# Two PSUM tiles for a pair's block products, a new list of steps, and the low parts of x2's sums on GpSimd

## The chip, the core and the metric

The kernel runs on one core of a Trainium2 chip. The metric is the device time in microseconds (us) from the first to the last instruction of the core and what lies around it; smaller is better. In the text PE is TensorE, DVE is VectorE, ACT is ScalarE, POOL is GpSimd, and SP is the engine whose queue issues every DMA of this kernel.

## What is computed

```python
def _moe_ref(x, w_in, w_out):            # 4608 x 512, 512 x 2048, 2048 x 512
    h = x @ w_in
    g = h - np.tanh(h)
    return g @ w_out

def _moe2_ref(x, w_in, w_out, a, b):     # same shapes
    h = x @ w_in
    h2 = h * h
    P = a[0] + a[1] * h + a[2] * h2 + a[3] * h2 * h
    Q = 1.0 + np.abs(b[0]) * np.abs(h) + np.abs(b[1]) * h2
    return (P / (Q + 1e-06)) @ w_out

x = attention(q, k, v)                   # linear attention, 8 x 8 heads, 576 x 64
return _moe2_ref(x=_moe_ref(x=x, ...), ...)
```

## The kernel before

Every large product is done in three matmuls of fp32r operands: each operand is split into a high part (a copy rounded to fp32r) and a low part (what is left), and high by high, high by low and low by high are added up in PSUM.

**The first phase** (the loop over `STEPS` = 144 steps, 9 blocks of 512 tokens with 16 slices of d_ff each) computes attention and the first feed-forward layer. A step does 12 matmuls for `hps`, then tanh on ACT, the subtraction on DVE, the high part on ACT (line 327), the low part on POOL (line 331), and two steps later 12 matmuls into four banks `acc`. The attention of the next block runs beside it in small pieces, among them a chain of K's column maxima (DVE, a DMA to HBM and back, DVE, ACT's exp, PE's `kvps`, line 490). At the end of a block its result x2 is cut into quadrants, and `x2_units` (lines 346 to 378) forms the seven sums that a 2 x 2 block product by Strassen-Winograd needs. Each of the seven is split: ACT copies the high part (line 356), an engine subtracts it from the sum in place to get the low part (line 357), and SP stores both to `x2d` in HBM (line 359). One piece of that generator runs per step. Line 357 is on DVE for units 1, 5, 7, 6 and 4, and on POOL for 3 and 2.

**The second phase** (the loop over `PAIRS` = 72 pairs of slices, 8 pairs to a block of tokens) computes the second layer. A pair `i` needs seven block products `P1` to `P7` (`product`, lines 814 to 833), each of 6 matmuls of 256 columns. They share one PSUM tile `zy` of two banks with four halves: product 4 in half 0, products 1, 6, 7 on top of each other in half 1 (one running sum), product 2 in half 2, products 5 and 3 on top of each other in half 3. ACT takes a copy of half 1 after product 1 (`s1`), after 6 (`s2`) and after 7 (`s3`, into `top`). DVE then forms the two slices of h: `add2` reads halves 0 and 3 plus `top` (side B of the pair), and `add1`, after product 3, reads halves 2 and 3 plus the two copies in `sums` (side A). The rational function of h follows for each side: `ab`, `sq`, `n1`, `rs`, `r2` on ACT, `q`, `st`, `en`, `gh`, `gl` on DVE, `m1`, `m2`, `m3` on POOL, `n0` on POOL (A) or ACT (B). `gh` and `gl` are the high and low parts of the result, and four groups `G` (`GA0` to `GA3`, `GB0` to `GB3`, 3 matmuls of 512 columns each) multiply them into the banks `acc0` to `acc3`. After 8 pairs `lv0` to `lv3` copy the banks out (DVE) and store them.

What sets the order in the second phase is the table `ORDER` (lines 28 to 39), written out by hand: each entry is a step and its lag. In round `i` the loop at line 992 emits the steps in that order, each for pair `i - lag`; every engine executes its own instructions in the order in which they are emitted. Waits between engines are set by the framework: a write to a PSUM tile waits for the reads of that tile that were emitted before it. `zy` has one buffer, so product 1 of a pair waits for all reads of the pair before.

The operands of the products stand in a ring: the weights of a pair are loaded after product 3 of the pair four before it (`ring`), and the units of x2 are loaded by `load_unit` at the last pair of a block, each into the place of the unit that the product just done has freed:

```python
if q == KF // 2 - 1:
    load_unit(*((j + 1, u + 3) if u < 4 else (j + 2, u - 4)))
```

`u` is the product's place in `UNITS = (1, 5, 2, 6, 7, 4, 3)`. So product 2 (`u` = 2) loads the unit that product 4 of the next block reads. The sums of the last block of x2 are formed in the second phase, one piece per round (`prep`, line 998).

Of the kernel before, what the change touches and what calls it, by code (L numbers as in the profile page):

```python
# [8 lines left out]
F32 = mybir.dt.float32  # L9
F32R = mybir.dt.float32r  # L10
# [5 lines left out]
ALU = mybir.AluOpType  # L16
AX = mybir.AxisListType

P = 128
# [10 lines left out]
    for name, lag in (  # L30
        x.split(".")
        for x in """
    P1.0 n0B.1 glB.2 m3A.2 P5.0 s1.0 lv2.3 stA.2 P2.0 abB.1 m1B.1 lv3.3 P6.0 enA.2 sqA.1 GB0.2 qB.1 s2.0
    n0A.1 GB2.2 ghA.2 rsB.1 P4.0 m2B.1 glA.2 r2B.1 P7.0 abA.1 GB1.2 stB.1 m3B.1 GB3.2 s3.0 qA.1 n1A.1
    GA1.2 add2.0 rsA.1 GA2.2 m1A.1 enB.1 GA0.2 sqB.0 ghB.1 P3.0 n1B.0 m2A.1 lv0.2 GA3.2 lv1.2 r2A.1
    add1.0
    """.split()
    )
]
LAGS = max(lag for _, lag in ORDER)  # L40
# [3 lines left out]
def attention_moe_moe2_kernel(ctx, tc, q, k, v, w1, w2, w3, w4, ca, cb, out):  # L44
# [145 lines left out]
    HALF = NB // 2  # L190
# [94 lines left out]
    def ring(i):  # L285

        h, l = wsl["a", i % (WS)]
        f = 2 * (i % (KF // 2))
        d = parked["a", f]
        SP.dma_start(out=f32(h), in_=d[:, 0:4])  # L290
        SP.dma_start(out=f32(l)[:, 0:3], in_=d[:, 4:7])

    def combo(i, m, c):

        u = UNITS.index(m)
        t = wsl["a", i % WS][u // 4][:, u % 4, :]
        return t[:, c * P:(c + 1) * P], t[:, HALF + c * P:HALF + (c + 1) * P]
# [45 lines left out]
    def two(t):  # L343
        return t.rearrange("p (c x) -> p c x", c=2)

    def x2_units(j, k0, k1, ta, tb, new_hi):

        x11, x12, x21, x22 = k0[:, :, LO], k0[:, :, HI], k1[:, :, LO], k1[:, :, HI]
        ta, tb = two(ta), two(tb)

        def minus(o, a, b):
            POOL.tensor_tensor(out=o, in0=a, in1=b, op=ALU.subtract)

        def split(m, x, eng):
            hi = two(new_hi())
            ACT.copy(out=hi.bitcast(F32R), in_=x)
            eng.tensor_tensor(out=x.bitcast(F32R), in0=x, in1=f32(hi), op=ALU.subtract)
            for i, t in enumerate((hi, x)):
                SP.dma_start(out=two(x2d[j][:, 2 * UNITS.index(m) + i]), in_=f32(t))

        minus(ta, x12, x11)
        yield
        split(1, x11, DVE)
        minus(tb, x22, ta)
        yield
        split(5, ta, DVE)
        minus(x12, x22, x12)
        yield
        split(3, x22, POOL)
        yield  # L370
        split(7, x12, DVE)
        minus(ta, x21, tb)
        yield
        split(2, x21, POOL)
        yield
        split(6, tb, DVE)
        yield
        split(4, ta, DVE)
# [319 lines left out]
    with tc.manual_schedule():  # L698
# [104 lines left out]
        def unit(j, m):  # L803
            k = 2 * (len(UNITS) * j + UNITS.index(m))
            return [units[(k + i) % len(units)] for i in range(2)]

        def load_unit(j, u):
            if j < NBLK:
                for i, t in enumerate(unit(j, UNITS[u])):
                    SP.dma_start(out=f32(t), in_=x2d[j][:, 2 * u + i])  # L810

        pair, tile = {}, {}

        def product(i, m):

            if m == 1:
                pair[i] = ps_p.tile([P, 4, HALF], F32, tag="zy", name="zy")
            o = pair[i][:, {1: 1, 6: 1, 7: 1, 4: 0, 2: 2, 5: 3, 3: 3}[m], :]
            j, q = i // (KF // 2), i % (KF // 2)
            hi, lo = unit(j, m)  # L820
            for c in range(2):
                wh, wl = combo(i, m, c)
                xc = slice(c * HALF, (c + 1) * HALF)
                for k, (w, x) in enumerate(((wh, hi), (wh, lo), (wl, hi))):
                    PE.matmul(  # L825
                        o, w, x[:, xc], start=m in (1, 5) and c == k == 0, stop=c == 1 and k == 2,
                        skip_group_check=True,
                    )
            u = UNITS.index(m)
            if q == KF // 2 - 1:  # L830
                load_unit(*((j + 1, u + 3) if u < 4 else (j + 2, u - 4)))
            if u == len(UNITS) - 1 and i + WS < PAIRS:
                ring(i + WS)

        def snap(i, k):
            ACT.copy(out=top if k == 2 else sums[:, k * HALF:(k + 1) * HALF], in_=pair[i][:, 1, :])  # L836

        def add1(i):
            zy = pair.pop(i)
            t = tile[2 * i] = {}  # L840
            new(t, "h")
            DVE.tensor_tensor(out=t["h"], in0=zy[:, 2:4, :].rearrange("p r x -> p (r x)"), in1=sums, op=ALU.add)  # L842

        def add2(i):
            zy = pair[i]
            t = tile[2 * i + 1] = {}
            new(t, "h")
            DVE.tensor_tensor(
                out=two(t["h"]), in0=zy[:, 0:4:3, :], in1=top.unsqueeze(1).to_broadcast([P, 2, HALF]), op=ALU.add
            )  # L850
# [51 lines left out]
        for n in range(STEPS):  # L902
# [9 lines left out]
            if n == last + 10:  # L912
# [10 lines left out]
                sums = xup.tile([P, NB], F32, tag="sums", name="sums")  # L923
                top = xup.tile([P, HALF], F32, tag="top", name="top")
# [10 lines left out]
            t = gp.tile([P, NB], F32, tag="t", name="t", bufs=1)  # L935
# [42 lines left out]
        steps = {f"P{m}": lambda i, m=m: product(i, m) for m in UNITS}  # L978
        steps |= {"s1": lambda i: snap(i, 0), "s2": lambda i: snap(i, 1), "s3": lambda i: snap(i, 2), "add1": add1, "add2": add2}
# [49 lines left out]
```

## Time and profile before

| what | value |
|---|---|
| median of 3 runs | 1789.42 us (1786.61 to 1790.46) |
| profiled execution | 1785.54 us, span 1783.8 us |
| PE busy | 1676.2 us, 94% of the span |
| DVE, ACT, POOL busy | 1177.7, 1010.1, 983.2 us |
| PE's clock over the span | 0.990 of full speed |
| first phase | from 0 to about 921 us |
| second phase | from about 921 us to the end |

A busy PE in this profile is not a PE at its peak, because matmuls are pipelined and their ends are modelled. The rate is read from the distance between starts; a gap stands in brackets behind a row with the engine and line that ended it.

### The profile page before, as it was taken

The page shows a single profiled execution, that of the slowest core. Times are in us where ns is not written, and L with a number is a line of the kernel's source. Part 1 is how long each engine was busy: PE and PEld are TensorE (multiplying, and loading weights), DVE is VectorE, ACT ScalarE, POOL GpSimd, SP SyncE. Part 2 cuts the span into 40 slices and gives each one's busy share as a digit, 9 for nine tenths or more (in the row PEclk, how much of TensorE's full clock was granted, in tenths as well). Part 3 has the DMA queues.
Part 4 walks back from the last instruction along what each step waited for, and adds up shares of the span by engine and source line. Part 5 has one row for each costly group of instructions (what it writes and reads, how often), then busy time and mean ns, then how long its engine had stood idle before and what let it go on. Part 6 is the DMA issues. An engine that isn't in the chain of part 4 may idle for free.

```text
span 1783.8 us, 25853 instructions
## 1 busy us (share of the span) xinstructions
PE 1676.2 (94%) x8776; PEld 1410.2 (79%) x8776; DVE 1177.7 (66%) x1921; ACT 1010.1 (57%) x1825; POOL 983.2 (55%) x830
## 2 busy tenths in 40 slices
PE   5899999999999999999998999999999999999998
PEld 4677787888878787888877878888888788888886
DVE  8987657666657666552216786767776767676776
ACT  5675444445444444443327766666666666666664
POOL 3223434443434444352427877777777777777775
PEclk8999999999999999999999999999999999999999
DMA  8553637565563737350786876666575748575630
GB/s 222 177 170 101 192 108 206 143 185 167 166 192 116 212 111 217 96 172 17 233 309 205 288 227 215 199 203 217 187 236 167 254 154 269 161 249 171 198 121 24
DMA packets 246115, 323.67 MB, mean 181 GB/s; under 512 B 119008, under 2 KB 176352, under 8 KB 236768
## 3 DMA queue, kind: packets, MB, share of 16 engines
q1 hardware_dynamic: 245984, 322.03, 57.7%
q8 instruction: 69, 1.13, 0.3%
q14 instruction: 62, 0.51, 0.1%
HBM read 249.04 MB, written 72.93 MB: 180 GB/s over the span
## 4 chain that ended last, share of the span: by engine, by line
PE 74%; DVE 12%; ACT 6%; DMA 3%; issue 3%; SPq 1%; POOL 1%; DVEq 0%; POOLq 0%; ACTq 0%
PE zy L825 21%; PE acc L80 11%; PE acc L81 11%; PE acc L82 11%; PE hps L80 5%; PE hps L82 5%; PE hps L81 5%; DVE h L842 3%; DMA ke<-kd 2%; ACT sums L836 2%; PE kvps L490 1%; DVE m L147 1%; DVE ke L473 1%; ACT m L133 1%; DVE m L134 1%
## 5 line engine op out<-in xcount | busy, mean ns | idle before, releaser
L331 POOL TENSOR_TENSOR gl<-t,gh 128x512 fp32r<-128x512 f32 x128 | 171.8, 1342 | 352.4 <-ACT gh L327 323.4
L327 ACT CAST gh<-t 128x512 fp32r<-128x512 f32 x128 | 79.6, 622 | 309.3 <-PE acc L82 129.2
L883 POOL TENSOR_TENSOR n<-n,r 128x512 f32<-128x512 f32 x144 | 186.8, 1297 | 101.6 <-ACT r L880 96.1
L883 POOL TENSOR_TENSOR n<-n,h 128x512 f32<-128x512 f32 x144 | 186.9, 1298 | 74.2 <-ACT n L863 62.6
L883 POOL TENSOR_TENSOR n<-n,n 128x512 f32<-128x512 f32 x144 | 186.4, 1294 | 5.7
L836 ACT COPY sums<-zy 128x256 f32<-128x256 f32 x144 | 53.6, 372 | 224.3 <-PE zy L825 222.2
L939 DVE TENSOR_TENSOR t<-hps,t 128x512 f32<-128x512 f32 x128 | 87.4, 683 | 119.9 <-ACT t L936 119.1
L936 ACT ACTIVATE t<-hps 128x512 f32<-128x512 f32 x144 | 85.8, 596 | 98.6 <-PE hps L82 80.6
L872 DVE SCALAR_TENSOR_TENSOR a<-h,absb,a 128x512 f32<-128x512 f32 x144 | 108.1, 751 | 46.0 <-ACT a L857 45.8
L886 DVE SCALAR_TENSOR_TENSOR a<-a,r 128x512 f32<-128x512 f32 x144 | 100.0, 694 | 47.6 <-ACT r L880 47.4
L842 DVE TENSOR_TENSOR h<-zy,sums 128x512 f32<-128x512 f32 x72 | 49.7, 690 | 104.8 <-ACT n L867 94.1
L863 ACT ACTIVATE n<-h,coef 128x512 f32<-128x512 f32 x144 | 117.1, 813 | 0.0
L889 DVE SCALAR_TENSOR_TENSOR a<-a,n 128x512 f32<-128x512 f32 x144 | 100.0, 694 | 9.5 <-POOL n L883 3.5
L893 DVE CAST gh<-a 128x512 fp32r<-128x512 f32 x144 | 99.1, 688 | 7.4
L896 DVE TENSOR_TENSOR gl<-a,gh 128x512 fp32r<-128x512 f32 x144 | 98.8, 686 | 7.0
L875 ACT ACTIVATE r<-a,bias_q 128x512 f32<-128x512 f32 x144 | 98.7, 686 | 4.0 <-DVE a L872 3.9
L857 ACT ACTIVATE a<-h,coef 128x512 f32<-128x512 f32 x144 | 98.8, 686 | 2.4 <-DVE gl L896 2.3
L598 POOL TENSOR_TENSOR qe<-qe,qs 128x512 f32<-128x512 f32 x36 | 38.0, 1056 | 99.4 <-DVE qs L597 99.4
L880 ACT ACTIVATE r<-r 128x512 f32<-128x512 f32 x144 | 90.3, 627 | 2.3
L860 ACT ACTIVATE h<-h 128x512 f32<-128x512 f32 x144 | 89.8, 624 | 0.8 <-DMA xl<-x2d 0.8
L869 POOL TENSOR_SCALAR n<-h,coef 128x512 f32<-128x512 f32 x72 | 55.5, 770 | 50.7 <-DVE a L889 50.7
L490 PE MATMUL kvps<-vt,ke 128*128 128x130 f32 x320 | 47.7, 300 | 27.1 <-ACT ke L483 25.8
(313 smaller groups left out, 5188.9 us busy)
## 6 DMA issues: line engine op xcount, KB each, us to landing
u<-x2d SPq DMA_DIRECT2D x78, 256.0 KB, 5.3
raw<-in_moe_w_in_dram SPq DMA_DIRECT2D x32, 512.0 KB, 4.5
raw<-in_moe_w_out_dram SPq DMA_DIRECT2D x32, 512.0 KB, 4.4
x2d<-e SPq DMA_DIRECT2D x56, 256.0 KB, 3.0
wa0h<-wa0d SPq DMA_DIRECT2D x9, 1024.0 KB, 5.1
wa1h<-wa2d SPq DMA_DIRECT2D x9, 1024.0 KB, 5.1
wa2h<-wa4d SPq DMA_DIRECT2D x9, 1024.0 KB, 5.1
wa3h<-wa6d SPq DMA_DIRECT2D x9, 1024.0 KB, 7.9
```

What stands on the lines that cost most here:

```text
L80: PE.matmul(o, lhi, rhi, start=start, stop=False)
L81: PE.matmul(o, lhi, rlo, start=False, stop=False)
L82: PE.matmul(o, llo, rhi, start=False, stop=stop)
L331: eng.tensor_tensor(out=gl, in0=g, in1=f32(gh), op=ALU.subtract)
L825: PE.matmul(o, w, x[:, xc], start=m in (1, 5) and c == k == 0, stop=c == 1 and k == 2, skip_group_check=True,)
L842: DVE.tensor_tensor(out=t["h"], in0=zy[:, 2:4, :].rearrange("p r x -> p (r x)"), in1=sums, op=ALU.add)
L863: ACT.activation(out=new(t, "n1"), in_=t["h"], func=AF.Identity, scale=a3, bias=a2)
L872: DVE.scalar_tensor_tensor(out=t["a"], in0=t["h2"], scalar=b1, in1=t["a"], op0=ALU.mult, op1=ALU.add)
L883: return lambda t: POOL.tensor_tensor(out=t[a], in0=t[a], in1=t[b], op=op)
L886: DVE.scalar_tensor_tensor(out=t["a"], in0=t["a"], scalar=ONE_EPS, in1=t["r"], op0=ALU.add, op1=ALU.mult)
L889: DVE.scalar_tensor_tensor(out=t["a"], in0=t["a"], scalar=2.0, in1=t["n0"], op0=ALU.subtract, op1=ALU.mult)
L893: DVE.tensor_copy(out=t["g"][0], in_=t["a"])
```

## The change

- The tile `zy` becomes two tiles of one bank each: `y` with product 4 in half 0 and products 5 and 3 in half 1, and `z` with product 2 in half 0 and products 1, 6, 7 in half 1. Products 2 and 4 change banks by this. `add2` reads `y` alone.
- `add1` becomes two instructions of 256 columns: `a11` (z plus the first copy) and `a12` (y plus the second).
- `ORDER` is laid out anew. The products now run 1, 6, 5, 4, 7, 2, 3 instead of 1, 5, 2, 6, 4, 7, 3. The eight groups stand in four twos, behind products 1, 7, 2 and 3. `GA3` and `GA0` have lag 3.
- Line 357 is on POOL for all seven units, in both phases.
- `prep` runs in every fourth round from round 3 on, instead of in each round from round 2 on. The load of the first block's last unit stands ahead of a weight load between the phases.

```diff
-    P1.0 n0B.1 glB.2 m3A.2 P5.0 s1.0 lv2.3 stA.2 P2.0 abB.1 m1B.1 lv3.3 P6.0 enA.2 sqA.1 GB0.2 qB.1 s2.0
...
+    P1.0 ghB.2 m3A.2 GA3.3 s1.0 glB.2 GA0.3 n1A.1 stA.2 P6.0 m1B.1 sqA.1 lv1.3 enA.2 P5.0 s2.0 ghA.2
...
-        def split(m, x, eng):
+        def split(m, x):
             hi = two(new_hi())
             ACT.copy(out=hi.bitcast(F32R), in_=x)
-            eng.tensor_tensor(out=x.bitcast(F32R), in0=x, in1=f32(hi), op=ALU.subtract)
+            POOL.tensor_tensor(out=x.bitcast(F32R), in0=x, in1=f32(hi), op=ALU.subtract)
...
             if m == 1:
-                pair[i] = ps_p.tile([P, 4, HALF], F32, tag="zy", name="zy")
-            o = pair[i][:, {1: 1, 6: 1, 7: 1, 4: 0, 2: 2, 5: 3, 3: 3}[m], :]
+                pair[i] = tuple(ps_p.tile([P, 2, HALF], F32, tag=tag, name=tag) for tag in "yz")
+            y, z = pair[i]
+            o = {1: z[:, 1], 6: z[:, 1], 7: z[:, 1], 2: z[:, 0], 4: y[:, 0], 5: y[:, 1], 3: y[:, 1]}[m]
...
-        def add1(i):
-            zy = pair.pop(i)
-            t = tile[2 * i] = {}
-            new(t, "h")
-            DVE.tensor_tensor(out=t["h"], in0=zy[:, 2:4, :].rearrange("p r x -> p (r x)"), in1=sums, op=ALU.add)
+        def add1(i, k):
+            t = tile.setdefault(2 * i, {})
+            h = t["h"] if t else new(t, "h")
+            c = slice(k * HALF, (k + 1) * HALF)
+            y, z = pair[i]
+            DVE.tensor_tensor(out=h[:, c], in0=y[:, 1] if k else z[:, 0], in1=sums[:, c], op=ALU.add)
...
-        ring(WS - 1)
         load_unit(0, 6)
+        ring(WS - 1)
...
-            if i >= LAGS:
+            if i % 4 == 3:
                 next(prep, None)
```

PE, second phase, a pair of the last block, before: the last group of the pair ahead (bank `acc_16533`), then the products 1 and 5 (one row, from `xh`), the products 2 and 6 (one row, from `xl`), and the first group behind them.

```order
L80 MATMUL acc_16533<-wb2h,gh 128x512
L81 MATMUL acc_16533<-wb2l,gh 128x512
L82 MATMUL acc_16533<-wb2h,gl 128x512
L825 MATMUL zy<-xh,wa3h 128x256 x12
L825 MATMUL zy<-xl,wa3h 128x256 x12
L80 MATMUL acc_16493<-wb2h,gh 128x512
```

The same place after: the group `GB0`, product 1, the groups `GA3` and `GA0`, product 6, product 5.

```order
L80 MATMUL acc_16697<-wb2h,gh 128x512
L81 MATMUL acc_16697<-wb2l,gh 128x512
L82 MATMUL acc_16697<-wb2h,gl 128x512
L826 MATMUL z<-xh,wa3h 128x256 x6
L80 MATMUL acc_16689<-wb2h,gh 128x512
L81 MATMUL acc_16689<-wb2l,gh 128x512
L82 MATMUL acc_16689<-wb2h,gl 128x512
L80 MATMUL acc_16697<-wb2h,gh 128x512
L81 MATMUL acc_16697<-wb2l,gh 128x512
L82 MATMUL acc_16697<-wb2h,gl 128x512
L826 MATMUL z<-xl,wa3h 128x256 x6
L826 MATMUL y<-xh,wa3h 128x256 x6
```

Two groups now stand between product 1 and the next product that writes the same tile, where another product of the same tile stood; between product 3 and the next product 1 there are two groups (of which the last is shown) instead of one.

DVE, one pair of the second phase, before (line 848 is `add2`, 842 `add1`, 872 `q`, 886 `st`, 889 `en`, 893 `gh`, 896 `gl`):

```order
L848 TENSOR_TENSOR h<-zy,top 128x512
L889 SCALAR_TENSOR_TENSOR a<-a,n_16585 128x512
L893 CAST gh<-a 128x512
L842 TENSOR_TENSOR h<-zy,sums 128x512
L896 TENSOR_TENSOR gl<-a,gh 128x512
L886 SCALAR_TENSOR_TENSOR a<-a,r 128x512
L889 SCALAR_TENSOR_TENSOR a<-a,n_16620 128x512
L872 SCALAR_TENSOR_TENSOR a<-h_16674,absb,a 128x512
L893 CAST gh<-a 128x512
L896 TENSOR_TENSOR gl<-a,gh 128x512
L886 SCALAR_TENSOR_TENSOR a<-a,r 128x512
L872 SCALAR_TENSOR_TENSOR a<-h_16731,absb,a 128x512
```

One pair on DVE after (line 844 is `a11` and `a12`):

```order
L848 TENSOR_TENSOR h<-y,top 128x512
L872 SCALAR_TENSOR_TENSOR a<-h_16853,absb,a 128x512
L844 TENSOR_TENSOR h<-z,sums 128x256
L886 SCALAR_TENSOR_TENSOR a<-a,r 128x512
L844 TENSOR_TENSOR h<-y,sums 128x256
L889 SCALAR_TENSOR_TENSOR a<-a,n_16883 128x512
L893 CAST gh<-a 128x512
L896 TENSOR_TENSOR gl<-a,gh 128x512
L886 SCALAR_TENSOR_TENSOR a<-a,r 128x512
L889 SCALAR_TENSOR_TENSOR a<-a,n_16874 128x512
L893 CAST gh<-a 128x512
L896 TENSOR_TENSOR gl<-a,gh 128x512
```

The one sum of 512 columns is two of 256, with `st` of side B between them, and the two sides' `en`, `gh`, `gl` stand in one run after them.

POOL, first phase, behind a block's end, as a piece of the difference (line 352 is a sum of `x2_units`, 357 a low part, 331 the low part of g, 598 a piece of attention):

```order
 L331 TENSOR_TENSOR gl<-t,gh 128x512
-L352 TENSOR_TENSOR xr<-raw,xr 128x512
-L598 TENSOR_TENSOR qe<-qe,qs 128x512
-L331 TENSOR_TENSOR gl<-t,gh 128x512
+L357 TENSOR_TENSOR raw<-raw,e 128x2x256
+L352 TENSOR_TENSOR xr<-raw,xr 128x512
+L598 TENSOR_TENSOR qe<-qe,qs 128x512
+L331 TENSOR_TENSOR gl<-t,gh 128x512
+L357 TENSOR_TENSOR xr<-xr,e 128x512
 L352 TENSOR_TENSOR raw<-raw 128x2x256
```

Two low parts have come in between the low parts of g.

## Rows read from the trace of the kernel before

**Rows 1.** Busy time by stretch: us, then each engine, clock, DMA share, GB/s.

```profile
700.00:800.00 100.00, 99.05 (x452) 82.19 (x451) 59.16 (x94) 47.22 (x86) 43.84 (x36) 1.00 0.47 145
956.66:1751.95 795.29, 749.36 (x4488) 644.21 (x4488) 565.64 (x854) 534.39 (x959) 583.41 (x483) 1.00 0.62 202
```

**Rows 2.** Waits from 850 us on: who waited for whom, us, times, longest.

```profile
PE zy L825 <- ACT sums L836: 34.1, 74, 0.5
PE zy L825 <- DVE h L842: 16.4, 71, 1.0
```

**Rows 3.** PE in order of time, one pair: start, us, line, operation, count, gap.

```profile
1305.91 0.87 PE L825 MATMUL zy<-u,wa0l 128*128 128x256 f32 x6
...
1307.08 0.39 PE L82 MATMUL acc<-wb3h,gl 128*128 128x512 f32 x1
1307.63 1.70 PE L825 MATMUL zy<-xl,wa1h 128*128 128x256 f32 x12 [0.16 <-DVE h L842]
1309.79 1.69 PE L825 MATMUL zy<-u,wa1h 128*128 128x256 f32 x12 [0.46 <-ACT sums L836]
1311.31 0.39 PE L80 MATMUL acc<-wb3h,gh 128*128 128x512 f32 x1
...
1312.70 1.58 PE L825 MATMUL zy<-u,wa1l 128*128 128x256 f32 x12
1314.12 0.40 PE L80 MATMUL acc<-wb3h,gh 128*128 128x512 f32 x1
```

**Rows 4.** The same stretch on DVE and ACT.

```profile
1306.89 0.69 DVE L842 TENSOR_TENSOR h<-zy,sums 128x512 f32<-128x512 f32 x1 [1.71 <-ACT n L867]
1309.37 0.37 ACT L836 COPY sums<-zy 128x256 f32<-128x256 f32 x1 [2.57 <-PE zy L825]
```

**Rows 5.** Groups by line from 850 us on: count, busy us, mean ns, idle before.

```profile
L883 POOL TENSOR_TENSOR n<-n,r 128x512 f32<-128x512 f32 x144 | 186.8, 1297 | 101.6 <-ACT r L880 96.1
L863 ACT ACTIVATE n<-h,coef 128x512 f32<-128x512 f32 x144 | 117.1, 813 | 0.0
L886 DVE SCALAR_TENSOR_TENSOR a<-a,r 128x512 f32<-128x512 f32 x144 | 100.0, 694 | 47.6 <-ACT r L880 47.4
```

**Rows 6.** PE in order of time: starts of pairs 1, 3, 71, and the end.

```profile
935.49 1.68 PE L825 MATMUL zy<-u,wa1h 128*128 128x256 f32 x12 [0.78 <-DVE h L842]
...
956.66 1.68 PE L825 MATMUL zy<-u,wa3h 128*128 128x256 f32 x12 [0.16 <-DVE h L842]
...
1751.95 1.69 PE L825 MATMUL zy<-xh,wa3h 128*128 128x256 f32 x12 [0.16 <-DVE h L842]
...
1761.88 0.87 PE L825 MATMUL zy<-u,wa3l 128*128 128x256 f32 x6
...
1777.68 0.39 PE L82 MATMUL acc<-wb3h,gl 128*128 128x512 f32 x1
```

**Rows 7.** Line 810, the unit loads after 900 us: time to landing.

```profile
DMA to landing us min/median/max: 2.7/5.2/9.8
```

**Rows 8.** Busy time of a stretch at a block's end, columns as in Rows 1.

```profile
1378.00:1399.00 21.00, 19.92 (x122) 17.38 (x123) 15.05 (x23) 14.33 (x27) 14.70 (x14) 1.00 0.95 333
```

**Rows 9.** Line 357 by engine and tile: duration ns min/median/max.

```profile
L357 DVE TENSOR_TENSOR xr<-xr,e x24: 679/694/1437, 174.7 to 884.6; 128x512 fp32r<-128x512 f32 x24
...
L357 DVE TENSOR_TENSOR raw<-raw,e x16: 940/1292/1776, 166.3 to 868.3; 128x512 fp32r<-128x512 f32 x16
L357 POOL TENSOR_TENSOR raw<-raw,e x16: 1263/1285/1745, 185.9 to 874.5; 128x512 fp32r<-128x512 f32 x16
```

**Rows 10.** SP's queue, DVE and PE around 190 us, in order of time.

```profile
187.18 0.37 SPq L359 DMA_DIRECT2D x2d<-raw  x1
187.64 0.42 SPq L538 DMA_DIRECT2D ke<-kd  x1
```

**Rows 11.** DVE and PE behind those two rows.

```profile
191.74 1.08 DVE L544 TENSOR_REDUCE mx<-ke 128x128 f32<-128x512 f32 x1 [2.35 <-DMA ke<-kd]
```

**Rows 12.** PE's longest wait behind that.

```profile
198.31 2.53 PE L490 MATMUL kvps<-vt,ke 128*128 128x130 f32 x10 [4.08 <-ACT ke L483]
```

More of the change, by code (lines that the diff above doesn't have):

```diff
@@ L32 @@
         for x in """
-    P1.0 n0B.1 glB.2 m3A.2 P5.0 s1.0 lv2.3 stA.2 P2.0 abB.1 m1B.1 lv3.3 P6.0 enA.2 sqA.1 GB0.2 qB.1 s2.0
-    n0A.1 GB2.2 ghA.2 rsB.1 P4.0 m2B.1 glA.2 r2B.1 P7.0 abA.1 GB1.2 stB.1 m3B.1 GB3.2 s3.0 qA.1 n1A.1
-    GA1.2 add2.0 rsA.1 GA2.2 m1A.1 enB.1 GA0.2 sqB.0 ghB.1 P3.0 n1B.0 m2A.1 lv0.2 GA3.2 lv1.2 r2A.1
-    add1.0
+    P1.0 ghB.2 m3A.2 GA3.3 s1.0 glB.2 GA0.3 n1A.1 stA.2 P6.0 m1B.1 sqA.1 lv1.3 enA.2 P5.0 s2.0 ghA.2
+    P4.0 abB.1 n0A.1 glA.2 P7.0 n0B.1 m1A.1 qB.1 GB2.2 lv3.3 s3.0 GB1.2 abA.1 lv0.3 add2.0 m2B.1 P2.0
+    rsB.1 qA.1 GA2.2 r2B.1 a11.0 GA1.2 sqB.0 stB.1 m3B.1 lv2.2 P3.0 n1B.0 GB3.2 a12.0 rsA.1 m2A.1 GB0.2
+    enB.1 r2A.1
     """.split()
@@ L362, in x2_units @@
         yield
-        split(1, x11, DVE)
+        split(1, x11)
         minus(tb, x22, ta)
         yield
-        split(5, ta, DVE)
+        split(5, ta)
         minus(x12, x22, x12)
         yield
-        split(3, x22, POOL)
+        split(3, x22)
         yield
-        split(7, x12, DVE)
+        split(7, x12)
         minus(ta, x21, tb)
         yield
-        split(2, x21, POOL)
+        split(2, x21)
         yield
-        split(6, tb, DVE)
+        split(6, tb)
         yield
-        split(4, ta, DVE)
+        split(4, ta)
     identity = const.tile([P, P], F32, name="identity")
@@ L835, in snap @@
         def snap(i, k):
-            ACT.copy(out=top if k == 2 else sums[:, k * HALF:(k + 1) * HALF], in_=pair[i][:, 1, :])
-        def add1(i):
-            zy = pair.pop(i)
-            t = tile[2 * i] = {}
-            new(t, "h")
-            DVE.tensor_tensor(out=t["h"], in0=zy[:, 2:4, :].rearrange("p r x -> p (r x)"), in1=sums, op=ALU.add)
+            ACT.copy(out=top if k == 2 else sums[:, k * HALF:(k + 1) * HALF], in_=pair[i][1][:, 1])
+        def add1(i, k):
[4 more added lines that the diff above has]
+            DVE.tensor_tensor(out=h[:, c], in0=y[:, 1] if k else z[:, 0], in1=sums[:, c], op=ALU.add)
         def add2(i):
-            zy = pair[i]
-            t = tile[2 * i + 1] = {}
-            new(t, "h")
+            h = new(tile.setdefault(2 * i + 1, {}), "h")
             DVE.tensor_tensor(
-                out=two(t["h"]), in0=zy[:, 0:4:3, :], in1=top.unsqueeze(1).to_broadcast([P, 2, HALF]), op=ALU.add
+                out=two(h), in0=pair[i][0], in1=top.unsqueeze(1).to_broadcast([P, 2, HALF]), op=ALU.add
             )
@@ L963, in attention_moe_moe2_kernel @@
         ps_p = ctx.enter_context(tc.tile_pool(name="ps_p", bufs=1, space=bass.MemoryType.PSUM))
+        load_unit(0, 6)
         ring(WS - 1)
-        load_unit(0, 6)
         for u in range(3):
@@ L978, in attention_moe_moe2_kernel @@
         steps = {f"P{m}": lambda i, m=m: product(i, m) for m in UNITS}
-        steps |= {"s1": lambda i: snap(i, 0), "s2": lambda i: snap(i, 1), "s3": lambda i: snap(i, 2), "add1": add1, "add2": add2}
+        steps |= {"s1": lambda i: snap(i, 0), "s2": lambda i: snap(i, 1), "s3": lambda i: snap(i, 2), "a11": lambda i: add1(i, 0), "a12": lambda i: add1(i, 1), "add2": add2}
         for side, X in enumerate("AB"):
```

## The prediction

> **What bounds the kernel now.** I read the busy times by stretch first. In the first phase PE is 99% busy over 100 us at the full clock, and in the second 749 of 795 us, also at the full clock; DVE, ACT and POOL have 566, 534 and 583 us of work there [rows 1]. So PE sets the time in both phases, and the question is what stops it. The list of waits gives two names for the second phase: `zy` waits for ACT's copies 74 times and for `add1` 71 times, about once a pair each [rows 2]. The timeline shows what they really cost, since the gap in brackets is measured from the modelled end of a pipelined matmul and is too short. From start to start, 12 matmuls of 256 columns take 1.42 us and six of 512 columns take 1.39 us when nothing stops them (1312.70 to 1314.12, 1311.31 to 1312.70). Products 1 and 5 take 2.16 us, and products 2 and 6 behind them 1.52 [rows 3]. So the copy costs 0.74 us, and 0.10 us to get going again. Product 1 starts 0.55 us behind the last matmul of a group where 0.23 would do, so `add1` costs 0.32 us.
>
> The reason stands in the rows of the other engines: the copy `s1` starts only when product 5 has ended, though product 1 was done 0.7 us before, and product 2 starts only when the copy has ended [rows 4], though it writes the other bank. Tracking is by tile, and `zy` is one tile.
>
> From pair 3 to pair 71 there are 68 periods in 795.29 us [rows 6], 11.70 us each.
>
> **The steady part of the second phase.** A pair is 42 matmuls of 256 columns (3.5 x 1.42 = 4.97 us) and eight groups, now in four twos of 1.39 us (5.56 us) [rows 3]: 10.53 us with no wait. That is 1.16 us less than 11.70, and 68 x 1.165 = **79.2 us**. Whether all of it comes is a question of slack, which I walked through for one pair, with product 1 starting at 0 and every piece at these lengths: P1 to 0.71, GA3 GA0 to 2.10, P6 to 2.81, P5 to 3.52, P4 to 4.23, P7 to 4.94, GB2 GB1 to 6.33, P2 to 7.04, GA2 GA1 to 8.43, P3 to 9.14, GB3 GB0 to 10.53. A reader of PSUM starts about 0.3 us behind the slot of the last matmul, and a copy takes 0.37 us [rows 3, 4].
> - `s1` ends at 1.38; product 6 wants it at 2.10. `s2` ends at 3.48; product 7 at 4.23. `s3` ends at 5.61; product 2 at 6.33. Each has 0.72 us to spare.
> - `add2` (0.69) ends at 6.35; product 3 wants `y` at 8.43. `a11` ends at about 7.75; the next product 1 at 10.53. `a12` ends at about 9.85; the next product 5 at 13.3. No row shows the 256-column addition; I take 0.4 us, between the copy's 0.37 and 0.69 for 512 columns [rows 4]. It is hidden at both.
> - Work per period is 8.3 us on DVE, 7.9 on ACT and 8.6 on POOL (565.6, 534.4 and 583.4 over 68) [rows 1], so 75 to 82% of 10.53. The second addition adds 0.1 us. The longest loop through the engines that I find is m3A, enA, ghA, glA, abA, rsB, r2B, sqB, n1B, rsA, r2A and m3A again: one step of 1.30 us on POOL, three of 0.69 on DVE, seven on ACT of at most 0.81 and, by its busy time, 0.68 on average [rows 5]: 8.1 us, 8.7 with hand-overs of 0.05. It closes within 10.53 with 1.8 us to spare. At a block's end `lv` puts up to three copies of some 0.7 us into DVE's row in one round; the walk then has product 3 waiting for nothing with about 0.5 us left.
>
> A rule of the Trainium skill bears on which wait is real. What the row shows: product 2 waits for a copy that reads the other bank [rows 3, 4]. The Trainium skill (PSUM — Partial Sum Buffer, "Summary: rules for kernel authors") has readers and matmuls kept apart by bank, not by tensor. By that rule the split alone, in the old order, would free product 2 and most of product 1, some 1.06 us a pair, and by the row nothing is freed as long as the tile is one; the change does both, so the sum is the same. No run here shows the split alone.
>
> **The start.** Before, pair 0's rounds are latency: pair 1 starts at 935.49 and pair 3 at 956.66 [rows 6], 21.2 us for two pairs of which one has no group. The walk without the waits gives about 3 us off pair 0 and 3 us off pair 1; pair 2 still waits for its first gh and gl. I take **-6 us** (0 to -9).
>
> **The end.** Pair 71 starts at 1751.95, its last product at 1761.88, the last matmul at 1777.68, and the span ends at 1783.8 [rows 6]. Pair 71's product 3 comes 1.5 us earlier in its pair. Behind it the element chain sets the time; now six groups instead of four follow the last `glA`, two more of 0.69 us, and one more round of POOL steps. I take +2 us for these, **+0.5** net (-2 to +4).
>
> **The units at a block's end.** Product 4's unit of the next block is loaded when product 2 of the last pair is done. Product 2 was third and is now sixth, so only 6.98 us lie between (7.04 to 10.53 + 3.52 = 14.05), where a pair and more did. The load leaves at about 7.7 us behind its twin. Landing takes 5.2 us at the median and 9.8 at most [rows 7], in a stretch in which the DMA engines are 95% busy at 333 GB/s [rows 8]. So it lands 1.1 us early or 3.5 us late. In between lies the backlog: the weights of the pair before (1.8 MB) and six units of 0.52 MB at that rate. Eight boundaries: **+4 us** (0 to +28).
>
> **POOL's low parts.** Forty of them (24 + 16) leave DVE in the first phase and cost POOL 1.285 us each [rows 9], 51 us of a POOL that is 44% busy [rows 1]. PE is stopped there by K's maxima: SP issues the fetch of `kd` right behind a store of a low part [rows 10], DVE waits for it until 191.74 [rows 11], and PE for the exp behind that until 198.31, 4.08 us, the second time at a low clock (2.53 us for ten matmuls) [rows 12]. That low part was already on POOL, and those ahead of it in the queue had 2 us and more to spare. I take **0** (-8 where DVE's relief shortens the chain, +10 where a store on the SP queue comes 1.3 us late at eight waits).
>
> DVE's low part takes 0.68 us alone and up to 1.78, and POOL's 1.26 to 1.75 [rows 9]. The Trainium skill (SBUF — State Buffer, "Who interferes with whom") says that a VectorE instruction with two SBUF inputs and a GpSimd one that reads SBUF shut each other out. By that rule the move takes collisions away and POOL's other steps gain; the rows agree, and the sum is the same.
>
> In the second phase five low parts move to POOL, one piece every fourth pair: 1.3 us more in a round where POOL has 1.9 us free. **0** (0 to +3). Moving the unit load past a weight load costs nothing: both are wanted later than pair 0's first products.
>
> **The sum**, against the profiled execution: 1785.54 - 79.2 - 6 + 0.5 + 4 = 1704.8 us. The median of the runs lies 3.9 us above that execution, so **1708 us**. Ends: 1694, with nothing late at the boundaries and the first phase faster; 1720 with the first phase slower.
>
> **The rivals.**
> - *A remainder of the waits.* The spare 0.72 us behind each copy holds only if ACT is free just then. Between `s2` and `s3` it has `abB` and n0B, 1.5 us, and ends some 0.4 us early; the walk goes by means. If one copy per pair comes half of today's wait too late (0.35 us), 68 pairs give +24: 1732; at 0.6 us, 1749. For it: three waits that must all be met. Against it: no engine over 82%.
> - *The units come late.* By the largest landing time each boundary stops PE for 3.5 us: 1732. For it: the saturated stretch [rows 8]. Against it: the median lands in time.
> - *Slower than before: the loop through the elements becomes the bound.* Its eleven steps would have to need over 11.7 us instead of 8.7, say because `n0A` on POOL waits for `enA`, and m2A, m3A behind it come late round after round. PE then waits in `ghA` for every pair. From 11.8 us on the kernel is slower; at 12.1 us it is 0.4 x 68 = 27 us slower, less the 1.5 at the start that remain: about 1815. Against it: the 3 us of hand-overs that this takes stand in no row.
> - *The change does nothing for PE*, because something other than the tile holds product 2 back. Then the new order still puts groups between, and PE's gaps would move behind them: within 0.2% of before only if all of it comes back.
>
> **How the numbers follow.** Forecast (1694 to 1720) 0.68; remainder of the waits 0.16; late units 0.10; slower 0.04; nothing gained 0.02. The range goes to 1738, which takes in the forecast, the late units and the lower half of the remainder. A difference under about 0.2% is one that a measurement of this kernel can't tell from none. Faster 0.94, same 0.02, slower 0.04.
>
> **What would show it.** In the profile after, 12 matmuls of 256 columns take 1.42 us everywhere in a steady pair, pairs start 10.5 us apart, PE has no wait for ACT's copies, and `z` and `y` waits are gone from the list. PE's rows at a block's first product 4 show whether its unit was late. I'm wrong if pairs start over 11 us apart, if a wait of `acc` for gh or gl appears once a pair, or if the first phase ends at another time than 921 us by more than 10 us.

## The result and the profile after

The changed kernel takes 1707.92 us (median of 4 runs, 1705.21 to 1709.69) where the kernel before, run beside it, takes 1788.01: a ratio of 0.955 with a 95% interval of 0.953 to 0.957. Its profiled execution took 1705.21 us, with a span of 1703.4 us; the prediction's sum for it was 1704.8. Cut at the same products, the spans compare so (us):

| stretch | before | after | difference | forecast |
|---|---|---|---|---|
| start to the first product of the second phase | 921.35 | 925.39 | +4.0 | 0 |
| from there to pair 3 | 35.31 | 30.86 | -4.45 | -6 |
| pair 3 to pair 71 | 795.29 | 715.14 | -80.15 | -79.2, and +4 for late units |
| pair 71 to the end | 31.85 | 32.0 | +0.15 | +0.5 |
| span | 1783.8 | 1703.4 | -80.4 | -80.7 |

The total is right, but two of its terms are not: 4 us that were expected at the boundaries of blocks did not come, and 4 us that were not expected came in the first phase. How much of the latter is the change's and how much scatter is taken up below, with the low parts.

PE of the changed kernel in order of time, the first products of the second phase, of pair 3 and of pair 71 (start, us, line, tile, count):

```profile
925.39 0.87 PE L826 MATMUL z<-u,wa0h 128*128 128x256 f32 x6
...
956.25 0.87 PE L826 MATMUL z<-u,wa3h 128*128 128x256 f32 x6
...
1671.39 0.88 PE L826 MATMUL z<-xh,wa3h 128*128 128x256 f32 x6
```

The 68 periods between the last two take 10.517 us each, against 11.70 in [rows 6]. One pair of the changed kernel on PE, which answers to [rows 3]:

```profile
1305.46 0.87 PE L826 MATMUL z<-u,wa0h 128*128 128x256 f32 x6
1306.17 0.87 PE L826 MATMUL y<-xl,wa0h 128*128 128x256 f32 x6
...
1308.29 0.39 PE L80 MATMUL acc<-wb1h,gh 128*128 128x512 f32 x1
...
1309.68 0.87 PE L826 MATMUL z<-u,wa0h 128*128 128x256 f32 x6
```

Six matmuls of 256 columns follow one another in 0.71 us, six of 512 in 1.39 us (1308.29 to 1309.68), and no row carries a gap. The waits of PE from 925 us on, which answer to [rows 2] (who waited for whom: us, times, longest):

```profile
PE acc L80 <- DVE gh L893: 3.0, 3, 1.1
PE z L826 <- ACT sums L837: 2.4, 2, 1.9
...
PE y L826 <- DMA u<-x2d: 0.2, 1, 0.2
```

Of the 74 waits for the copies into `sums` two are left; with two for `top` (1.0 us, not shown) they lie in the first three pairs. The 71 for the first addition are gone, and what is left for `gh` lies in the last 20 us. The last row is the units: one product 4 waited, 0.2 us.

In the first phase the waits grew. The first fence is the changed kernel, from 160 to 921 us, rows of DVE, ACT, PE and SP's queue; the second is the same stretch with one thing undone, the low parts back on DVE (the run e3 below):

```profile
DVE mx L544 <- DMA ke<-kd: 57.7, 20, 4.8
ACT qh L635 <- DMA ql<-qd: 29.4, 17, 3.3
PE kvps L490 <- ACT ke L483: 16.6, 6, 4.0
...
SPq L359 <- POOL raw L357: 36.6, 20, 5.4
SPq L359 <- POOL xr L357: 17.4, 13, 3.6
```

```profile
DVE mx L544 <- DMA ke<-kd: 18.0, 14, 3.9
...
PE kvps L490 <- ACT ke L483: 14.2, 8, 4.0
...
SPq L359 <- POOL raw L357: 15.9, 12, 5.3
SPq L359 <- DVE xr L357: 9.4, 15, 1.6
SPq L359 <- DVE raw L357: 9.0, 9, 1.1
```

SP waits 54 us for low parts, all of them on POOL, before it can issue their stores; in e3 it waits 34 us, 16 for those on POOL and 18 for those on DVE. Two engines wait longer for fetches that SP issues behind those stores: DVE for `kd`, and ACT for `ql` (13.6 us in e3). PE's own waits for `kvps` grew less, from 14.2 to 16.6 us.

### The profile page after: what moved, and what is told of

Same layout as the page of the kernel before. It is cut to its first block, busy times and chain, and to the rows that moved or that the text cites. A ratio compares the mean times of both kernels' runs of the same rounds, so it can differ in the third digit from the quotient of the medians.

```text
span 1703.4 us, 25967 instructions
## 1 busy us (share of the span) xinstructions
PE 1644.1 (97%) x8776; PEld 1414.4 (83%) x8776; DVE 1154.1 (68%) x1948; ACT 1024.3 (60%) x1825; POOL 1035.3 (61%) x875
## 4 chain that ended last, share of the span: by engine, by line
PE 75%; DVE 9%; DMA 5%; ACT 4%; issue 3%; POOL 2%; SPq 2%; ACTq 0%; POOLq 0%; DVEq 0%
PE acc L80 12%; PE acc L81 12%; PE acc L82 12%; PE z L826 12%; PE y L826 9%; PE hps L80 5%; PE hps L82 5%; PE hps L81 5%; DMA ke<-kd 2%; PE kvps L490 1%; DMA u<-x2d 1%; SPq L629 1%; DVE m L147 1%; DMA ql<-qd 1%; ACT m L133 1%
## 5 line engine op out<-in xcount | busy, mean ns | idle before, releaser
L837 ACT COPY sums<-z 128x256 f32<-128x256 f32 x144 | 53.9, 374 | 134.0 <-PE z L826 134.0
L490 PEld LDWEIGHTS kvps<-vt,ke 128*128 128x128 f32 x320 | 44.9, 212 | 35.2 <-ACT ke L483 31.7
L636 DVE TENSOR_TENSOR ql<-ql,qh 128x512 fp32r<-128x512 f32 x28 | 23.5, 841 | 74.2 <-ACT qh L635 74.2
```

Source lines behind the costliest of these rows:

```text
L490: PE.matmul(ps[:, 0:2 * (D + 1)], e[:, g].rearrange("p h d -> p (h d)"), vs[:, :, g, :], start=g == 0, stop=g == G - 1,)
```

## The experiments

The theory after the result: the split into two tiles gives the steady gain, the low parts on POOL cost the first phase some us through SP's queue, and the units have time enough. The rival for the steady part was that the new list of steps earns it, since it puts other work behind each product that a copy reads. The kernel before was run beside each group of runs, at 1783.4 to 1784.9 us.

**The changed kernel once more**, as the measure for the rest.

> The changed kernel again, on the same chip as the next three, as their common mark. Both theories: 1708 us, within 4. Theory (low parts on POOL lengthen the first phase): its first product of the second phase starts at 925 us again, where the kernel before had 921. Rival (the 4 us were scatter of one execution): it starts anywhere from 920 to 927.

Measured: 1704.29 us (1700.68 to 1711.2), ratio 0.955 (0.953 to 0.958). Runs below are compared with this one.

**The split alone, in the old list.** The kernel before, with two tiles and the old halves in them, and `add2`, which then reads both tiles, as two additions of 256 columns.

```diff
-                pair[i] = ps_p.tile([P, 4, HALF], F32, tag="zy", name="zy")
+                pair[i] = tuple(ps_p.tile([P, 2, HALF], F32, tag=tag, name=tag) for tag in "zy")
...
+            o = {1: z[:, 1], 6: z[:, 1], 7: z[:, 1], 4: z[:, 0], 2: y[:, 0], 5: y[:, 1], 3: y[:, 1]}[m]
...
-                out=two(t["h"]), in0=zy[:, 0:4:3, :], in1=top.unsqueeze(1).to_broadcast([P, 2, HALF]), op=ALU.add
+            for k, part in enumerate((z[:, 0], y[:, 1])):
+                DVE.tensor_tensor(out=two(t["h"])[:, k], in0=part, in1=top, op=ALU.add)
```

> The kernel before with two one-bank tiles and nothing else: products 4, 1, 6, 7 in the one, 2, 5, 3 in the other, as the halves lay before; the old list of steps, low parts of x2 as before. The sum of side B now reads two tiles, so it is two additions of 256 columns. Theory (tracking by tile holds PE; the rule by banks): product 2 no longer waits for the copy, product 6 finds it done, product 1 no longer waits for add1 and product 5 behind it finds it done, so pairs start 10.5 us apart, as in the changed kernel, and the time is 1704, between 1698 and 1712. Rival (the new list, with groups between the products, is what frees PE): the gaps stay or move to products 6 and 4, pairs 11.4 to 11.7 us apart, 1770 to 1785.

Measured: 1698.79 us, ratio 0.952 (0.949 to 0.954). PE in its steady part, products 1, 5, 2 and 6:

```profile
1307.03 0.88 PE L826 MATMUL z<-xl,wa1h 128*128 128x256 f32 x6
1307.74 0.88 PE L826 MATMUL y<-xl,wa1h 128*128 128x256 f32 x6
1308.46 0.87 PE L826 MATMUL y<-u,wa1h 128*128 128x256 f32 x6
1309.17 0.87 PE L826 MATMUL z<-u,wa1h 128*128 128x256 f32 x6
```

Product 2 follows product 5 at once, where [rows 3] had 0.74 us between. Pairs 3 and 71 start at 947.44 and 1664.02 us: 10.54 us a pair, 1.16 less than before. The split alone does it. That this kernel is 5.5 us below the changed one goes with its low parts, which are still on DVE: e3, with the new list and the same low parts, takes 1697.68 us. The result agrees with the rule of the Trainium skill that the prediction weighed (PSUM — Partial Sum Buffer, "Summary: rules for kernel authors"), by which a reader and the matmuls that run beside it belong in different banks, with waits kept bank by bank.

**The list alone, in one tile.** The changed kernel with `y` and `z` as the halves of one tile.

```diff
-                pair[i] = tuple(ps_p.tile([P, 2, HALF], F32, tag=tag, name=tag) for tag in "yz")
+                t = ps_p.tile([P, 4, HALF], F32, tag="zy", name="zy")
+                pair[i] = t[:, 0:2], t[:, 2:4]
```

> The changed kernel with its four halves in one tile again (z its first bank, y its second), list of steps and low parts as changed. Theory (tracking by tile): by the walk the copy behind product 6 now waits for product 5 too, and product 4 waits for that copy, 0.67 us and 0.1 to get going; product 2 and product 1 of the next pair find their readers just done. Pairs start 11.2 to 11.4 us apart, 1750 to 1765. Rival (the list alone frees PE): 10.5 us, 1704. Rival (the list does nothing without the tiles): 11.6 us or more, 1780 and up.

Measured: 1766.17 us, ratio 0.990 (0.987 to 0.993). Its waits from 925 us on, and PE at products 5, 4 and 7 of a pair (its lines from 818 on stand one further down):

```profile
PE zy L827 <- ACT sums L838: 34.3, 74, 0.5
...
PE zy L827 <- DVE h L845: 2.1, 4, 0.6
```

```profile
1301.09 0.87 PE L827 MATMUL zy<-xl,wa1h 128*128 128x256 f32 x6
1302.42 1.68 PE L827 MATMUL zy<-u,wa1l 128*128 128x256 f32 x12 [0.46 <-ACT sums L838]
```

The list takes the wait for the first addition away and leaves the one for the copy, 74 times as before, now at product 4: 1301.09 to 1302.42 is 1.33 us for a product of 0.71. Pairs are 11.36 us apart, 0.34 less than before, close to the 0.32 that the prediction had put on `add1`.

**The low parts.** Line 357 of the changed kernel on the engines of before, and the kernel before with all of line 357 on POOL.

```diff
-        split(1, x11)
+        split(1, x11, DVE)
...
-            POOL.tensor_tensor(out=x.bitcast(F32R), in0=x, in1=f32(hi), op=ALU.subtract)
+            eng.tensor_tensor(out=x.bitcast(F32R), in0=x, in1=f32(hi), op=ALU.subtract)
```

> The changed kernel with the low parts of units 1, 5, 7, 6, 4 back on DVE in both phases; the rest as changed. Theory (POOL's low parts hold SP's queue and so the fetches behind it, and read SBUF against DVE): 4 us less than the changed kernel, about 1704, with the first product at about 921; SP's waits for line 357 on POOL back from 54 us to about 16. Rival (scatter): 1708, no difference beyond the interval. What I forecast before the result, zero with -8 to +10, lies between.

> The kernel before with nothing changed but the low parts of x2's sums, all on POOL. Theory: 4 us more than before, about 1792, first product at about 925. Rival (scatter): same as before, 1788. In its second phase the pieces still run once a pair in pairs 2 to 9, with five low parts of 1.29 us more on POOL, whose spare time there is 3 us a pair: no difference by either.

Measured: 1697.68 us with the low parts back on DVE, 6.6 us less than the changed kernel; 1793.96 us for the kernel before with them on POOL (ratio 1.0047, 1.0032 to 1.0063), 10 more than before, where 4 had been expected by the theory. Where it is lost shows in the starts of the steps' tanh (ACT, line 936; 144 of them), as us behind the same step of e3:

| step | before | split alone | changed | changed again | before, lows on POOL |
|---|---|---|---|---|---|
| 70 | 1.7 | -1.5 | 0.8 | -0.5 | -1.9 |
| 76 | 1.9 | -1.5 | 3.9 | 2.6 | 1.9 |
| 100 | 2.7 | -1.6 | 3.6 | 1.2 | -0.4 |
| 108 | 3.0 | -2.3 | 6.9 | 5.7 | 3.0 |
| 144 | 3.0 | -2.3 | 7.1 | 5.9 | 3.2 |

All three executions with the low parts on POOL lose 3 to 4.5 us from step 70 to 76 and again from 100 to 108; none with them on DVE does. Of the first loss they keep 1.5 to 2.8 us at step 100. From step 70 to 144 they lose 5.1 to 6.4 us against e3, and two more executions with these parts on POOL (the runs with the list alone and with the units later, below) 4.2 and 5.0; the kernel before loses 1.3, and the split alone gains 0.8.

The end of the first phase tells less, since it scatters: the kernel before and the split alone have the same first phase and reach the first product of the second at 921.35 and 916.01 us, e3 at 918.32. The five with the low parts on POOL reach it at 921.50 to 925.39, and the lowest of these is the kernel before with the parts moved, whose expectation had 925. So the 4.0 us of the table above are, by themselves, no more than this scatter; the 6.6 us between the medians and the stretches from step 70 on are the evidence. The second place in the changed kernel, rows of POOL, SP, ACT, DVE and PE in the order in which they depend on each other:

```profile
667.62 1.21 POOL L245 TENSOR_TENSOR m<-m 128x256 f32<-128x256 f32 x1
668.78 1.29 POOL L357 TENSOR_TENSOR raw<-raw,e 128x512 fp32r<-128x512 f32 x1
...
670.10 0.37 SPq L359 DMA_DIRECT2D x2d<-raw  x1
670.58 2.69 SPq L629 DMA_DIRECT2D ql<-qd  x4
...
675.68 0.63 ACT L635 CAST qh<-ql 128x512 fp32r<-128x512 f32 x1 [1.79 <-DMA ql<-qd]
...
679.26 0.29 DVE L530 TENSOR_REDUCE mc<-mx 128x4 f32<-128x128 f32 x1
...
696.67 1.54 PE L490 MATMUL kvps<-vt,ke 128*128 128x130 f32 x10 [3.34 <-ACT ke L483]
```

and in e3:

```profile
660.85 1.29 DVE L357 TENSOR_TENSOR raw<-raw,e 128x512 fp32r<-128x512 f32 x1 [0.58 <-ACT e L356]
...
662.17 0.37 SPq L359 DMA_DIRECT2D x2d<-raw  x1
662.65 2.69 SPq L629 DMA_DIRECT2D ql<-qd  x4
...
672.88 0.29 DVE L530 TENSOR_REDUCE mc<-mx 128x4 f32<-128x128 f32 x1
...
690.57 1.38 PE L490 MATMUL kvps<-vt,ke 128*128 128x130 f32 x10 [1.66 <-ACT ke L483]
```

On POOL the low part stands behind a string of weight-decoding steps (lines 242 to 245), of which the last is shown. SP can't issue the store before it is done: the store comes 5.7 us behind that of the high part (664.37 on SP), where e3 has 1.4 (660.77). The fetch of Q behind it leaves at 670.58. ACT waits for it, DVE's next maxima of K come behind ACT, and PE's `kvps` waits twice as long.

In the run on the kernel before, the profiled execution had another loss as well, at the start of the second phase, where its expectation had no difference. Busy time by stretch, from the first product to pair 3 (us; PE, PEld, DVE, ACT, POOL; clock; DMA share; GB/s), of that run, of the changed kernel, and of e3:

```profile
921.50:962.00 40.50, 34.18 (x175) 29.43 (x173) 15.48 (x24) 21.93 (x39) 17.73 (x15) 0.79 0.70 253
```

```profile
925.39:956.25 30.86, 27.46 (x170) 24.73 (x169) 15.24 (x25) 21.27 (x38) 17.10 (x15) 0.94 0.85 321
```

```profile
918.32:947.63 29.31, 25.91 (x169) 23.19 (x168) 15.05 (x26) 21.39 (x38) 16.80 (x14) 1.00 0.88 337
```

The granted clock is 0.79 in the first, which takes 40.5 us where before took 35.31 at 1.00: 5 of the 6 us by which the span of this execution exceeds that of before. PE's waits in it are no longer than before (6.5 us by the brackets, against 6.9), so why the clock fell is open, and the loss is not shown to come from the low parts. Its twelve runs go from 1784.9 us at a clock of 0.992 over the span to 1797.33 at 0.984, so part of the 10 us hangs on the clock. The changed kernel loses 1.5 us of this kind against e3; for that too the low parts are not shown to be the cause (below, on the start).

**The fetch of `kd` ahead of the stores.** The changed kernel, with the fetch emitted in the step before; and the same with the low parts on DVE.

```diff
-    KV_LATER = (kv_max, kv_squares, kv_fetch, kv_join, kv_sub, kv_exp, (kv_mm, kv_norm))
+    KV_LATER = (kv_max, kv_squares, (lambda b, p: None, kv_fetch), kv_join, kv_sub, kv_exp, (kv_mm, kv_norm))
...
-                for fn, s in zip(KV, (0, 1, 2, 3, 3)) if j == 1 else zip(KV_LATER, (-2, -2, 2, 3, 3, 4, 4)):
+                for fn, s in zip(KV, (0, 1, 2, 3, 3)) if j == 1 else zip(KV_LATER, (-2, -2, 1, 3, 3, 4, 4)):
```

> The changed kernel with the fetch of K's maxima (line 538) issued at the end of the step before, ahead of that step's stores of x2's units on SP's queue, instead of behind them. Theory (in the first phase PE waits for exp because the fetch stands behind stores that wait for low parts): DVE's wait for the fetch (57.7 us, 20 times after 160 us) falls to under 20, PE's waits of line 490 for exp after 160 us (16.6 us in seven) to under 6, and with the low clock behind them gone the kernel takes 12 to 18 us less, about 1693. Rival (DVE's and ACT's own rows set the time of exp, whatever the fetch does): under 4 us less.

> Two edits together, for a faster version: the fetch of K's maxima ahead of the stores, and the low parts back on DVE, on the changed kernel. Theory (both act on the same wait, the fetch's landing, which the first edit has removed): little of the 6.6 us of the second edit is left, 1686 to 1690. Rival (they act on different waits, the second through POOL's and DVE's rows): the full sum, about 1683.

> The changed kernel with the early fetch once more, beside the split in the old list on the same chip: 1687 to 1693 us. If the new list is worth something by itself it is the faster of the two by more than 4 us; if not, they differ by less than 4 us.

Measured: 1690.18 and, once more, 1689.66 us (ratio 0.947, 0.945 to 0.948), 14 us less than the changed kernel; 1689.96 with the low parts on DVE, so with this fetch early nothing is left of their 6.6 us. Waits of the first of these, 160 to 921 us:

```profile
DVE mx L544 <- DMA ke<-kd: 4.5, 7, 0.8
...
PE kvps L490 <- ACT ke L483: 1.3, 2, 1.1
```

The wait for `kd` is nearly gone and with it 15 us of PE's waiting. Most of that is older than the change: e3 has 14.2 us of it, and [rows 10 to 12] show one such wait. What the wait costs beside its own length is seen at the place of [rows 12] in the changed kernel and, behind it, in this one:

```profile
199.49 2.54 PE L490 MATMUL kvps<-vt,ke 128*128 128x130 f32 x10 [4.00 <-ACT ke L483]
```

```profile
194.72 1.38 PE L490 MATMUL kvps<-vt,ke 128*128 128x130 f32 x10 [0.24 <-ACT ke L483]
```

The same ten matmuls take 1.16 us more behind 4 us of idling: the granted clock is 0.50 while they run, and 1.00 in the second row. What is not gone is ACT's wait for `ql`: it has grown from 29.4 us to 61.9, in 22 places.

**The fetch of Q ahead too, and alone.** The four DMAs of line 629 are emitted one step earlier in the same way.

```diff
-    Q_LATER = (q_max, q_sub, q_exp, q_sum, q_squares, q_fetch, q_split, (q_mm, q_out))
+    Q_LATER = (q_max, q_sub, q_exp, q_sum, q_squares, (lambda j, p: None, q_fetch), q_split, (q_mm, q_out))
...
-            for fn, s in zip(Q, (-1, 0, 1, 2, 4, 5)) if j == 1 else zip(Q_LATER, (-3, -2, -1, 0, 1, 3, 4, 5)):
+            for fn, s in zip(Q, (-1, 0, 1, 2, 4, 5)) if j == 1 else zip(Q_LATER, (-3, -2, -1, 0, 1, 2, 4, 5)):
```

> The changed kernel with both fetches early: the one of kd as in the run before, and the four DMAs of the fetch of qd (line 629), which stood on the SP queue behind a store of a low part, now ahead of that round's stores. Theory (the low parts on GpSimd hold up whatever SP issues behind their stores, and the fetch of qd is what is still held up with the kd fetch moved: ScalarE waits 62 to 64 us in 22 places for ql there, up to 6 us): those waits fall under 20 us. What that gives in time is bounded by what TensorE still loses between 160 and 907 us, 747 less 740 us: 2 to 6 us, so 1684 to 1688 against 1690 us. Rival (ScalarE's wait is not on the path of TensorE, or SP now waits for TensorE's reads of ql and holds up the rest): 1689 us or more.

> The changed kernel with the fetch of qd alone moved ahead, the one of kd left behind the stores. In the trace of the changed kernel the store at 670.10 us waits for a low part behind four other steps on GpSimd, the fetch of qd behind it leaves at 670.58, ScalarE waits for it until 675.68, VectorE's next maxima of K come behind that, and TensorE waits 3.34 us at 696.67 where the kernel with the low parts on VectorE waits 1.66. Theory: this part of the loss goes, 2 to 4 us, so 1700 to 1702 us against 1704.3, with ScalarE's waits for ql under 15 us instead of 29; the waits for kd stay near 57 us. Rival (it all hangs on the fetch of kd): 1703 to 1706 us.

Measured: 1683.61 us with both fetches early (ratio 0.943, 0.942 to 0.944), the best of all kernels here, 20.7 us below the changed one; 1697.56 with Q's fetch alone, 6.7 below. Both gained more than their expectations said. With both early, from 160 to 921 us:

```profile
PE kvps L490 <- ACT ke L483: 4.1, 2, 3.1
...
ACT qh L635 <- DMA ql<-qd: 0.7, 2, 0.4
...
SPq L629 <- PE xps L82: 25.1, 8, 6.3
```

SP now waits 25 us for PE's reads of `ql`, and still ACT hardly waits for `ql`, nor DVE for `kd` (3.2 us). Neither of the two places of the low parts loses time any more against e3 (from step 70 to 76 -0.2 us, from 100 to 108 -1.5). With Q's fetch alone the places still lose 1.4 and 2.2 us, with `kd`'s alone (the repeat) 2.3 and 2.9: both hang on both fetches. What Q's fetch alone gains comes mostly before step 92, so that its 6.7 us equal the 6.6 of the low parts is a coincidence.

**The old list with the early fetch**, to see what the new list is worth: the kernel before with the split alone and the fetch of `kd` early. Its low parts are where they were before.

> Before with three edits: the split into two one-bank tiles in the old list of steps, the low parts where they were before (DVE for five units), and the fetch of kd emitted one step earlier, ahead of the stores of x2's sums. Theory (the split alone gives the steady gain, the early fetch alone the gain of the first phase, and the two don't touch): 1698.8 less 7 to 14 us, 1684 to 1692 us, the first product of the second phase at 908 to 912 us, pairs 10.5 us apart. Rival (the new list earns something that the noise of the first phase hid in the earlier run): 1694 us or more, with pairs over 10.6 us apart or a longer end.

Measured: 1692.68 us, ratio 0.948 (0.947 to 0.950), 3.0 us above the changed kernel with the same fetch run beside it. Its pairs take 10.54 us, and those of the other 10.52, which is 1 us over 68 pairs. The spans of the profiles differ by 1.5 us: 0.8 in the first phase, 0.6 from there to pair 3, 1.0 in the steady pairs, less 0.9 at the end. Two executions of the changed kernel with this fetch differ by 0.8 us over the steady pairs themselves. By the expectation, under 4 us is no gain of the list; whether it is worth 3 us or nothing stays open. It is not where the 80 us come from.

**The units later.** The changed kernel, with the unit that product 2 frees loaded behind product 3's.

```diff
-                load_unit(*((j + 1, u + 3) if u < 4 else (j + 2, u - 4)))
+                for u2 in {2: [], 6: [6, 2]}.get(u, [u]):
+                    load_unit(*((j + 1, u2 + 3) if u2 < 4 else (j + 2, u2 - 4)))
```

> The changed kernel with the unit that product 4 of the next block reads loaded behind product 3 of the last pair and behind that product's own unit, 2.1 us and one pair of transfers later. My sum had this unit land 1.1 us early at the median and late at the largest landing time, 0.5 us a boundary; the profile shows 0.2 us in all. By 1.1 us of slack: each of eight boundaries now stops PE about 1 to 2.5 us at product 4, 8 to 20 us more than the changed kernel, 1712 to 1724. Rival (the backlog at the boundary is smaller than I took it, and the unit lands 3 us or more early): within 3 us of the changed kernel.

Measured: 1719.14 us, ratio 0.964 (0.961 to 0.967), 14.9 us above the changed kernel. Its waits from 925 us on:

```profile
PE y L826 <- DMA u<-x2d: 6.3, 8, 2.1
...
PE y L826 <- DMA xh<-x2d: 2.4, 3, 1.5
```

Product 3 ends 2.10 us behind product 2 in the walk and the second load stands behind a first, and that delay is enough to make product 4 wait at seven of the eight boundaries. With 1.1 us for `xl` the waits add up to 9.8 us; the rest of the 14.9 is not broken down here. So the units arrive in time in the changed kernel, but with little to spare.

## Why the prediction was right, and where it wasn't

- **The steady part**: right. 68 periods of 10.517 us against 10.53 forecast; the walk's 0.72 us behind each copy held, and the rival with a remainder of the waits has no row. The addition of 256 columns took 0.42 us where 0.4 was taken. The loop through the elements didn't bind.
- **What gives it**: the prediction left open whether the split alone would do. It does (10.54 us a pair in the old list), and frees 1.16 us, a little more than the 1.06 that the text worked out; the list alone frees 0.34.
- **The start**: -4.45 against -6. The term was right for a PE at the full clock: e3, with the same code in this stretch, takes 29.31 us there, exactly 6.0 less than before. But pair 2 does not wait for its first gh and gl, as the prediction had it. Its product 6 waits for the copy `s1`, which ACT starts only at 945.81, behind elements that it works on from 941.20 without a gap: in this one pair ACT was not free, as the rival with a remainder of the waits had it. Behind that wait the granted clock falls, to 0.50 from 947.10 to 949.66:

```profile
946.22 1.08 PE L826 MATMUL z<-u,wa2h 128*128 128x256 f32 x6 [1.91 <-ACT sums L837]
947.10 1.49 PE L826 MATMUL y<-u,wa2h 128*128 128x256 f32 x6
948.38 1.48 PE L826 MATMUL y<-u,wa2l 128*128 128x256 f32 x6
```

  Two products take 1.28 us from start to start instead of 0.71, and the start is 1.5 us longer than in e3. The wait alone doesn't bring this price. The same place with both fetches early:

```profile
926.44 0.97 PE L826 MATMUL z<-u,wa2h 128*128 128x256 f32 x6 [1.90 <-ACT sums L837]
927.25 0.87 PE L826 MATMUL y<-u,wa2h 128*128 128x256 f32 x6
927.96 0.87 PE L826 MATMUL y<-u,wa2l 128*128 128x256 f32 x6
```

  All nine runs with the new list in two tiles have this wait of 1.9 us. Six of them took 30.8 to 30.9 us from the first product to pair 3. The other three took 29.3 at a clock of 1.00: e3, the same kernel with the fetch of `kd` early, and the run shown, whose low parts are on POOL. What decides between the two isn't shown.
- **The units at a block's end**: mis-sized, 0.2 us over all boundaries against +4. The 9.8 us of landing behind "3.5 us late" do not belong to the boundaries: the loads of [rows 7] that are issued up to 960 us, between the phases, land in 5.1 to 9.8 us, and those from 960 us on in 2.7 to 7.1. In the changed kernel they land in 3.3 to 6.5 us from 960 to 1660 us. A load that leaves at 7.7 in the walk and takes 6.5 is some 0.15 us late, which is about the 0.2 that one boundary shows. (The distance from 7.04 to 14.05 is 7.01 us, not 6.98; nothing hangs on it.) The run with the later load shows that the caution was about a real edge.
- **The end**: +0.15 against +0.5.
- **The low parts on POOL**: the step that failed. The prediction took 0, since the one low part that it looked at was on POOL already "and those ahead of it in the queue had 2 us and more to spare". The runs show 6.6 us between the medians with and without the move (first phase and start together, and the 1.5 us of the start are not shown to belong to it). The way was the one named with the bound of +10, a store on the SP queue that comes late; but it was not eight times the 1.3 us of POOL's own work. At the places that cost, the low part stands behind four decode steps on POOL, its store leaves 4.2 and 5.7 us behind that of the high part, where e3 has 1.0 and 1.4, and what stands behind that is also Q's fetch, which the prediction hadn't looked at.
- **The sum**: that it came out to 0.4 us is luck. The +4 of the units, which did not come, stood in for what came in the first phase and was not in the sum.

## What to carry to other kernels

Where a matmul waits for a reader of another bank, ask first whether the wait is by tile: one tile for each bank gave here what a new order of the work alone could not. When work moves to an engine with time to spare, look at what that engine has queued ahead of it at that moment, and at everything that is issued behind its result on a shared queue; the mean load tells neither. A fetch that someone waits for belongs ahead of stores that nobody waits for yet: moving two of them gave 20.7 us, in a phase in which PE was busy for 729 of 747 us (160 to 907 us of the changed kernel).

## What the chip showed beside that

- The price of a wait on PE can be more than its length, but need not be. Behind 4.00 us of idling ten matmuls took 2.54 us at a granted clock of 0.50, and behind 0.24 us 1.38 at 1.00. Behind 1.91 us at the start of the second phase two products took 1.28 us each at 0.50, and behind 1.90 us at the same place in another run 0.71 at 1.00.
- Two operations met that had not met before. DVE and POOL of the changed kernel, the exponent's input `ke` (two inputs in SBUF) and a low part, at the first of the two places:

```profile
508.44 1.95 DVE L473 TENSOR_TENSOR ke<-kt,mx 128x640 f32<-128x640 f32 x1
```

```profile
508.41 1.30 POOL L357 TENSOR_TENSOR xr<-xr,e 128x512 fp32r<-128x512 f32 x1
```

  Line 473 takes 0.83 us at the median and took 0.95 at that place in e3. The Trainium skill (SBUF — State Buffer, "Who interferes with whom") has such a pair shut each other out, and the trace agrees. The engines' rows lead from there to PE: DVE's next work, among it the input of ACT's next step, starts late, ACT's exp comes behind that at 513.12, and `kvps` waits 3.10 us for it (1.50 in e3). So the move to POOL did not only take collisions away, as the prediction had it; it also made one on PE's path. What this one costs by itself, beside the late fetches, isn't separated.
